# A table of rows in PSUM, a third step shared by two engines, and matrices made inside another step

## The chip, the cores and the metric

The kernel runs on one core of a Trainium2 chip. The core has a matrix engine (TensorE, "PE" in the profile), three engines for elementwise work (VectorE "DVE", ScalarE "ACT", GpSimd "POOL") and an engine whose queue here issues nearly all transfers (SyncE, "SP"). Matrix products land in PSUM, a small memory of eight banks; GpSimd does not touch it in this program. The metric is the time of one execution on the device, in microseconds. The program has one launch and computes everything from the raw inputs.

## The reference

Two blocks follow each other. The first is a long convolution over a sequence of 12480 positions, for a batch of 4 and 128 channels, done in the reference by FFT. The second is a feed-forward block over the 49920 rows that come out of it.

```python
h_mlp = np.maximum(pos_emb @ w1, 0.0) @ w2
h_filt = h_mlp * np.exp(-0.01 * pos)[:, None]
u = x * v
y = irfft(rfft(u, n=2*S) * rfft(h_filt, n=2*S))[:, :S, :]
attn = x * y                              # (4, 12480, 128)
x2 = attn.reshape(4 * 12480, 128)
h = x2 @ w_in                             # 128 -> 2048
out = (h * np.cos(h)) @ w_out             # 2048 -> 128
```

All values are float32.

## The kernel before

**The convolution.** The sequence is laid out as 104 rows (R) of 120 columns (N2), and the two transforms are products with small matrices of cosines and sines. For each of the four batch members there are four steps. In the forward first step (f1_units) and second step (f2_units) the product of x and v is transformed and multiplied with the filter. The third step (i1_units, 64 units) starts the way back. The fourth, the last inverse (i2_units), works in 30 groups (NG) of four columns: for each column two matrices of 96x104 stand against the third step's result in `slots`, and the product with x gives four columns of output rows, `zs`, which go to DRAM as `zd`.

**The third step.** One unit is four matmuls of 120x120 (L476, two records each) into one of eight banks, and its eviction i1_evict (L481). ScalarE copies half of the bank to SBUF (`other`, L484, a pool of two buffers); VectorE then writes the sum and the difference of the bank's other half and that copy to `slots` (L486, two instructions). Every inverse matmul of the fourth step reads all 64 units, so the fourth step cannot start before the last eviction.

For the first batch member the third step runs before the feed-forward block has begun, in the function `beside`: it is a generator that yields 130 times, and at every 14th yield a piece of w_out is converted from float64 words to float32 (convert_units: VectorE, GpSimd and ScalarE by turns), at every other fifth yield one matrix of the fourth step is made (some_groups).

**The matrices of the fourth step.** The two matrices of a column n2 are a rotation of the same table `rows` (96 x 4 x 104) by that column's cosine and sine from `tw_t` (make_t L305, turn L282). ScalarE writes the first term (L291). Then either VectorE adds the second term in one instruction (L293, scalar_tensor_tensor), or ScalarE writes the second term to `spare` (L296) and GpSimd adds the two (L297). make_group (L642) makes the four columns of a group and stores them to DRAM (`td`), where the other three batch members load them. For the first member, the groups in `SOME` (2, 7, 12, 17, 22, 27) are made by some_groups beside the third step, all on ScalarE and GpSimd, and loaded later; the other 24 are made within the fourth step, one group ahead of their use, two columns by VectorE (even ones) and two by GpSimd (odd ones). Group 0 is made when some_groups ends and advances the fourth step's generator once (L657).

**The feed-forward block** runs in 98 blocks of up to 128 x 4 rows with 16 steps each (1568 MoE steps). A step is a matmul up (L737, to a bank `ph` of four), then ScalarE `a` (L740), VectorE `k` (L743), GpSimd `f` (L746), ScalarE `cs` (L751), VectorE `gt` (L753), and four steps later a matmul down (L762, into `acc`). The cosine is made by `k`, `f` and `cs`.

**The order.** Nothing is reordered by a scheduler: every engine gets its instructions in the order in which the Python code emits them. The main loop emits a MoE step and then as many parts of the convolution's generators as fit its price (`owed`); one part of the first member's fourth step costs 0.875 MoE steps, a group has four parts, so groups carry 3 or 4 MoE steps by turns. `units` (L524) lays out a group: at part 0 the first half of its matmuls, the eviction of the group before, and the first column of the next group; at part 2 the second half. Beside it u_units of the next batch member runs (loads of x and v, L392, L398).

PSUM after the third step: one bank for `acc`, four for `ph`, three (`ps_c`) for the convolution.

Of the kernel before, what the change touches and what calls it, by code (L numbers as in the profile page):

```python
# [30 lines left out]
def kernel(  # L31
# [272 lines left out]

    def make_t(t, n2, **how):  # L305


        i = 1 if n2 < H - 1 else 0
        turn(t, rows[:, i:i + 2, :], rows[:, i + 1:i + 3, :], tw_t[:, 0, n2:n2 + 1],
             tw_t[:, 1, n2:n2 + 1], **how)  # L310
# [169 lines left out]

    def i1_evict(pool, ps, b):  # L481
        pj = ps[0:N1, 0:4 * N2].rearrange("p (i r j) -> p r j i", i=2, r=2)
        other = pool.tile([N1, N2, 2], F32, name="other")
        nc.scalar.copy(out=other[:, :, :], in_=pj[:, 1])  # L484
        for h, op in ((0, ALU.add), (1, ALU.subtract)):
            nc.vector.tensor_tensor(slots[0:N1, b, h * N2:(h + 1) * N2, :], pj[:, 0],  # L486
                                    other[:, :, :], op=op)
            yield
# [14 lines left out]

    def i2_out(pool, ps, xs, b, g):
        zs = pool.tile([R, 2, UA, D], F32, name="zs")
        nc.vector.tensor_tensor(
            zs[:, :, :, :].rearrange("p h n d -> p (h n d)"), ps[0:R, :],
            xs[:, :, :].rearrange("p h n -> p (h n)"), op=ALU.mult)
# [7 lines left out]
        yield  # L516

    made = [0]
    zbs = {}
# [3 lines left out]

    def units(n, steps, before, mm, after, parts, ahead=2):  # L524


        for j in range(min(ahead, n)):
            for _ in before(j) or ():
                pass
        yield 0.0  # L530
        last = iter(())
        for j in range(n):
            early = iter(before(j + ahead) or () if j + ahead < n else ())
            now = None
# [12 lines left out]
        for _ in last:  # L547
            pass
        yield REST

    SOME = range(2, NG, 5)
    REST = 3.0
# [77 lines left out]

    def i1_units(bank):
        with tc.tile_pool(name="mid", bufs=2) as pool:
            def mm(j, ps, i):
                if i == 0:
                    ps = bank()
                i1_mm(ps, j, i)
                return ps

            yield from units(CB, I1_STEPS, lambda j: None, mm,
                             lambda j, ps: i1_evict(pool, ps, j), 2)  # L640

    def make_group(pool, g, t, summed):  # L642

        for i, n2 in enumerate(n2s(g)):
            if summed < G and i % 2 == 0:
                make_t(t[:, i, :, :], n2)
            else:
                spare = pool.tile([N1, 2, R], F32, name="spare", bufs=2)
                make_t(t[:, i, :, :], n2, spare=spare[:, :, :])
            yield  # L650
        nc.sync.dma_start(td[g, :, :, :, :], t[:, :, :, :])

    def some_groups(pool):
        for g in SOME:
            t = pool.tile([N1, G, 2, R], F32, name="some", bufs=2)
            yield from make_group(pool, g, t, G)
        next(backs[0])  # L657

    def i2_units(bank, b, bufs):

        with tc.tile_pool(name="back", bufs=2, side="left" if b else "right") as pool:
# [10 lines left out]
            def mm(j, ps, i):  # L672
                if i == 0:
# [120 lines left out]
    with tc.manual_schedule():  # L794
        with tc.tile_pool(name="psum", bufs=8, space=PSUM) as psum, \
# [104 lines left out]
            nc.sync.dma_start(w_in_sb[:, :], wind[:, :])  # L900
            beside(i1_units(bank), [(w_out_sb[:, c, :], w) for c, w in out_pieces], some_groups)

        ps_acc = ctx.enter_context(tc.tile_pool(name="ps_acc", bufs=1, space=PSUM))
        ps_h = ctx.enter_context(tc.tile_pool(name="ps_h", bufs=4, space=PSUM))
        ps_c = ctx.enter_context(tc.tile_pool(name="ps_c", bufs=3, space=PSUM))
        mpool = ctx.enter_context(tc.tile_pool(name="moe", bufs=2))

        def bank():
            return ps_c.tile([P, BANK], F32, name="cv")
# [77 lines left out]
```

## Time and profile before

| What | us |
|---|---|
| median of four runs | 3773.79 (3771.79 to 3775.56) |
| the profiled execution: its time | 3772.35 |
| the profiled execution: its span | 3770.6 |
| third step of the first batch member (first to last matmul) | 272.7 to 333.5 |
| first inverse matmul | 338.3 |
| first matmul of the feed-forward block | 344.4 |
| last zs of the first member's fourth step starts | 586.5 |
| first matmul of the second member's forward step | 615.3 |

The span is what the profiler recorded on the core; the run's time is 1.75 us longer. A busy TensorE is not TensorE at its peak, since ends of matmuls are modelled: a record of 512 columns reads 592 ns, but in the chain of waits two of them take 0.86 us. float32 matmuls leave two records each.

The groups of the profile that the change touches, with the whole run's means:

| line, engine, what | count | mean ns |
|---|---|---|
| L486 VectorE, third step's sums and differences (first member) | 128 | 396 |
| L484 ScalarE, `other` (first member) | 64 | 346 |
| L293 VectorE, matrices within the fourth step | 48 | 941 |
| L297 GpSimd, matrices within the fourth step | 48 | 776 |
| L297 GpSimd, matrices beside the third step | 24 | 640 |
| L291 and L296 ScalarE, matrices | 192 | 455 to 468 |

### The profile page before, as it was taken

What the parts mean: (1) busy time and instruction counts of PE and PEld (TensorE: products, weight loads), DVE (VectorE), ACT (ScalarE), POOL (GpSimd) and SP (SyncE); (2) the same over time, 40 slices, a digit from 0 to 9 for tenths busy, and PEclk for the clock granted to TensorE, in tenths of its full rate; (3) what the DMA queues carried; (4) which work ended last, traced back from release to release, by engine and by line L of the source; (5) the groups of instructions that cost most, each with busy time, mean ns of one, the idle gap of its engine ahead of it and who ended that gap; (6) DMA issues with size and microseconds to landing.
All of it is one profiled execution on the core that took longest, in us unless ns stands there. A gap on an engine that the chain in (4) does not pass through costs nothing.

```text
span 3770.6 us, 47191 instructions
## 1 busy us (share of the span) xinstructions
PE 3692.9 (98%) x13546; PEld 2109.1 (56%) x13546; DVE 2779.2 (74%) x5562; ACT 2518.0 (67%) x4683; POOL 2570.3 (68%) x2342
## 2 busy tenths in 40 slices
PE   7898999999999999999999999999999999999999
PEld 6777555655566555555565556555566544444444
DVE  7887887688866777788766786788765566666666
ACT  5757776766665557766655567666664677777777
POOL 7667776588854665688745664788644577777776
PEclk9999999999999999999999999999999999999999
DMA  6263541022202550122103540122105200000000
GB/s 166 65 184 106 150 148 57 18 71 79 75 18 69 178 159 28 33 78 79 57 18 111 177 123 20 49 79 75 41 14 173 81 23 17 17 23 17 17 23 13
DMA packets 209499, 276.14 MB, mean 73 GB/s; under 512 B 17112, under 2 KB 146536, under 8 KB 209112
## 3 DMA queue, kind: packets, MB, share of 16 engines
q1 hardware_dynamic: 209239, 273.12, 24.5%
q8 instruction: 109, 1.79, 0.2%
q14 instruction: 151, 1.23, 0.1%
HBM read 193.64 MB, written 79.42 MB: 72 GB/s over the span
## 4 chain that ended last, share of the span: by engine, by line
PE 85%; DVE 4%; POOL 3%; DMA 3%; ACT 2%; issue 2%; SPq 0%; POOLq 0%; DVEq 0%; ACTq 0%
PE ph L737 33%; PE acc L762 28%; PE cv L501 5%; PE cv L762 5%; PE cv L476 4%; PE cv L445 3%; PE cv L404 3%; PE ph L126 2%; POOL f L746 2%; DMA hd<-h 2%; PE ps L404 1%; DMA tm<-td 1%; DVE slots L486 1%; ACT cs L751 1%; DVE gt L753 1%
## 5 line engine op out<-in xcount | busy, mean ns | idle before, releaser
L746 POOL TENSOR_TENSOR f<-a,k 128x512 f32<-128x512 f32 (+1 forms) x1568 | 1985.8, 1267 | 1059.9 <-DVE k L743 1056.0
L737 PE MATMUL ph<-at,w_in_sb 128*128 128x512 f32 (+1 forms) x3136 | 1599.0, 591 | 8.3 <-DVE gt L753 7.5
L740 ACT ACTIVATE a<-ph,quarter 128x512 f32<-128x512 f32 (+1 forms) x1568 | 1071.3, 683 | 687.2 <-PE ph L737 677.6
L762 PE MATMUL acc<-gt,w_out_sb 128*128 128x512 f32 (+1 forms) x2688 | 1370.0, 591 | 0.0
L753 DVE TENSOR_TENSOR gt<-ph,cs 128x512 f32<-128x512 f32 (+1 forms) x1568 | 1077.0, 687 | 368.6 <-ACT cs L751 353.4
L751 ACT ACTIVATE cs<-f 128x512 f32<-128x512 f32 (+1 forms) x1568 | 981.1, 626 | 385.5 <-POOL f L746 383.0
L743 DVE TENSOR_SCALAR k<-a 128x512 f32<-128x512 f32 (+1 forms) x1568 | 797.8, 509 | 545.3 <-ACT a L740 531.4
L762 PEld LDWEIGHTS acc<-gt,w_out_sb 128*128 128x128 f32 x2688 | 508.5, 189 | 642.0 <-issue 630.7
L737 PEld LDWEIGHTS ph<-at,w_in_sb 128*128 128x128 f32 x3136 | 553.0, 190 | 342.2 <-issue 261.6
L471 POOL TENSOR_TENSOR slots<-slots,t 120x256 f32<-120x256 f32 x384 | 311.3, 816 | 61.8 <-DVE t L464 25.8
L501 PEld LDWEIGHTS cv<-slots,tm 96*104 96x104 f32 x1920 | 239.6, 170 | 113.6 <-issue 84.3
L501 PE MATMUL cv<-slots,tm 96*104 96x128 f32 x1920 | 254.6, 274 | 13.7 <-DMA tm<-td 5.7
L762 PE MATMUL cv<-gt,w_out_sb 128*128 128x512 f32 (+1 forms) x448 | 224.6, 584 | 0.7 <-DVE gt L753 0.7
L476 PEld LDWEIGHTS cv<-cs,slots 120*96 120x96 f32 x1536 | 176.7, 167 | 67.6 <-issue 65.4
L476 PE MATMUL cv<-cs,slots 120*96 120x120 f32 x1536 | 183.1, 266 | 0.0
L445 PE MATMUL cv<-slots,w 124*120 124x256 f32 x576 | 173.1, 381 | 0.0
L445 PEld LDWEIGHTS cv<-slots,w 124*120 124x120 f32 x576 | 103.7, 184 | 123.7 <-issue 112.0
L404 PEld LDWEIGHTS cv<-c,slots 104*124 104x124 f32 x768 | 132.6, 192 | 71.2 <-issue 58.3
L404 PE MATMUL cv<-c,slots 104*124 104x192 f32 x768 | 151.2, 327 | 4.8 <-DVE gt L753 3.5
L762 PEld LDWEIGHTS cv<-gt,w_out_sb 128*128 128x128 f32 x448 | 84.9, 190 | 104.4 <-issue 99.4
L392 DVE TENSOR_TENSOR xt<-xt,vt 104x256 f32<-104x256 f32 x177 | 134.2, 761 | 0.2 <-DMA vt<-in_v_dram 0.2
L486 DVE TENSOR_TENSOR slots<-cv,other 96x240 f32<-96x240 f32 x384 | 133.1, 394 | 1.5 <-ACT other L484 1.4
(129 smaller groups left out, 2546.0 us busy)
## 6 DMA issues: line engine op xcount, KB each, us to landing
h<-hd SPq DMA_DIRECT2D x144, 240.0 KB
tm<-td SPq DMA_DIRECT2D x96, 312.0 KB
xt<-in_x_dram SPq DMA_DIRECT2D x120, 208.0 KB
vt<-in_v_dram SPq DMA_DIRECT2D x120, 208.0 KB
xs<-in_x_dram SPq DMA_DIRECT2D x120, 208.0 KB
zd<-zs SPq DMA_DIRECT2D x119, 208.0 KB
zb<-zd SPq DMA_DIRECT2D x96, 256.0 KB
w<-wd SPq DMA_DIRECT2D x144, 116.2 KB
```

Source lines behind the costliest of these rows:

```text
L404: nc.tensor.matmul(ps[0:KE, i * 2 * N1:(i + 1) * 2 * N1], u[:, b, 0:KE, i], c1[0:u.shape[0], :, :].rearrange("p r k -> p (r k)"), start=Tr ...
L445: nc.tensor.matmul(pi, w[:, i, :], parts[0:KE, :, k], start=True, stop=True)
L471: nc.gpsimd.tensor_tensor(y[:, r], y[:, r], t[:, r], op=op)
L476: nc.tensor.matmul(ps[0:N1, (i * 2 + r) * N2:(i * 2 + r + 1) * N2], parts[0:N2, r, :, b, i], cs[:, r, :], start=True, stop=True)
L501: nc.tensor.matmul(ps[0:R, i * D:(i + 1) * D], t[:, i, r, :], slots[0:N1, :, place, :], start=(r == 0), stop=(r == 1))
L737: nc.tensor.matmul(ph[:, 0:m], w_in_sb[:, c * P:(c + 1) * P], ats[n][:, 0:m], start=True, stop=True)
L740: nc.scalar.activation(a[:, 0:m], ph[:, 0:m], AF.Identity, bias=quarter[:, 0:1], scale=INV_TWO_PI)
L743: nc.vector.tensor_scalar(out=k[:, 0:m], in0=a[:, 0:m], scalar1=ROUND, scalar2=ROUND, op0=ALU.add, op1=ALU.subtract)
L746: nc.gpsimd.tensor_tensor(f[:, 0:m], a[:, 0:m], k[:, 0:m], op=ALU.subtract)
L751: nc.scalar.activation(cs[:, 0:m], f[:, 0:m], AF.Sin, scale=TWO_PI)
L753: nc.vector.tensor_tensor(gt[:, 0:m], ph[:, 0:m], cs[:, 0:m], op=ALU.mult)
L762: nc.tensor.matmul(accs[n][:, 0:m], w_out_sb[:, c, :], gt[:, 0:m], start=(c == 0), stop=(c == NFC - 1))
```

## The change

Six things are changed together.

- A copy of `rows` is put into a PSUM bank of its own by ScalarE, after the third step. make_t takes the second operand of VectorE's instruction from it, for the columns that VectorE makes. GpSimd's and ScalarE's part still reads SBUF. Group 0 is made before the copy exists and reads SBUF.
- That bank comes from the convolution's three, which has two until the first member's fourth step is over; then the table's pool is closed and three banks are opened.
- In the third step of the first member, units 58, 60 and 62 are evicted by GpSimd: ScalarE copies both halves of the bank to SBUF (`other` and `base`), GpSimd adds and subtracts. The other units stay as they were. i1_units of the later members passes no `last` and is unchanged.
- `SOME` has every seventh group (2, 9, 16, 23), four in place of six. Within the fourth step of the first member VectorE makes the odd columns and GpSimd the even ones.
- Before the last of the four groups, some_groups advances the fourth step's generator five times, so that group 0's four columns are made one by one within the third step. Conversions come at every 13th yield. To allow this, `units` yields while it prepares the first group, and inverse_units passes these yields on.
- In the first member's fourth step a group's matmuls come at parts 1 and 3 (`skip=1`), and its eviction one part later.

The program as a whole gets 3 `base` copies and one table copy on ScalarE, 6 adds on GpSimd in place of 6 on VectorE, 8 matrices made within the fourth step in place of beside the third, 50 of 52 L293 on tm with the PSUM operand, and 2 loads of `tm` fewer. The matmuls are the same.

```diff
-    def make_t(t, n2, **how):
+    def make_t(t, n2, copies=(), **how):
         i = 1 if n2 < H - 1 else 0
-        turn(t, rows[:, i:i + 2, :], rows[:, i + 1:i + 3, :], tw_t[:, 0, n2:n2 + 1],
+        second = rows
+        if copies:
+            second = copies[0]
+        turn(t, rows[:, i:i + 2, :], second[:, i + 1:i + 3, :], tw_t[:, 0, n2:n2 + 1],
              tw_t[:, 1, n2:n2 + 1], **how)
...
-    def i1_evict(pool, ps, b):
+    def i1_evict(pool, ps, b, gpsimd=False):
         pj = ps[0:N1, 0:4 * N2].rearrange("p (i r j) -> p r j i", i=2, r=2)
         other = pool.tile([N1, N2, 2], F32, name="other")
         nc.scalar.copy(out=other[:, :, :], in_=pj[:, 1])
+        first, engine = pj[:, 0], nc.vector
+        if gpsimd:
+            base = pool.tile([N1, N2, 2], F32, name="base")
+            nc.scalar.copy(out=base[:, :, :], in_=first)
+            first, engine = base[:, :, :], nc.gpsimd
         for h, op in ((0, ALU.add), (1, ALU.subtract)):
-            nc.vector.tensor_tensor(slots[0:N1, b, h * N2:(h + 1) * N2, :], pj[:, 0],
-                                    other[:, :, :], op=op)
+            engine.tensor_tensor(slots[0:N1, b, h * N2:(h + 1) * N2, :], first,
+                                 other[:, :, :], op=op)
             yield
...
     def i2_out(pool, ps, xs, b, g):
+        if b == 0:
+            yield
...
-    def units(n, steps, before, mm, after, parts, ahead=2):
+    def units(n, steps, before, mm, after, parts, ahead=2, skip=0):
         for j in range(min(ahead, n)):
             for _ in before(j) or ():
-                pass
+                yield 0.0
...
-                if i == 0 or 2 * i == max(parts, 2):
-                    now = mm(j, now, min(i, 1))
+                if i == skip or 2 * (i - skip) == max(parts, 2):
+                    now = mm(j, now, int(i > skip))
...
-    SOME = range(2, NG, 5)
+    SOME = range(2, NG, 7)
...
-                             lambda j, ps: i1_evict(pool, ps, j), 2)
+                             lambda j, ps: i1_evict(pool, ps, j, j >= CB - last and j % 2 == 0), 2)
...
-            if summed < G and i % 2 == 0:
-                make_t(t[:, i, :, :], n2)
+            if summed < G and i % 2:
+                make_t(t[:, i, :, :], n2, copies=rows_psum)
...
         for g in SOME:
+            if g == SOME[-1]:
+                for _ in range(G + 1):
+                    next(backs[0])
+                    yield
             t = pool.tile([N1, G, 2, R], F32, name="some", bufs=2)
             yield from make_group(pool, g, t, G)
-        next(backs[0])
...
-                             4 if b == 0 else 2, ahead=bufs - 1)
+                             4 if b == 0 else 2, ahead=bufs - 1, skip=int(b == 0))
...
-        for i, steps in enumerate(i2_units(bank, b, 2)):
+        back = i2_units(bank, b, 2)
+        for _ in range(0 if b else G):
+            yield next(back)
+        for i, steps in enumerate(back):
...
-                        if i % 14 == 0:
+                        if i % 13 == 0:
...
-            beside(i1_units(bank), [(w_out_sb[:, c, :], w) for c, w in out_pieces], some_groups)
+            beside(i1_units(bank, 6), [(w_out_sb[:, c, :], w) for c, w in out_pieces], some_groups)
...
-        ps_c = ctx.enter_context(tc.tile_pool(name="ps_c", bufs=3, space=PSUM))
+        stack = ctx.enter_context(ExitStack())
+        table_pool = stack.enter_context(tc.tile_pool(name="ps_t", bufs=1, space=PSUM))
+        two_banks = stack.enter_context(tc.tile_pool(name="ps_c", bufs=2, space=PSUM))
+        ps_c = [two_banks]
+        table = table_pool.tile([P, BANK], F32, name="table")
+        table = table[0:N1, 0:4 * R].rearrange("p (q n) -> p q n", q=4)
+        nc.scalar.copy(out=table, in_=rows[:, :, :])
+        rows_psum.append(table)
...
                 yield from backs[b]
+                if b == 0:
+                    stack.close()
+                    ps_c[0] = stack.enter_context(
+                        tc.tile_pool(name="ps_c", bufs=3, space=PSUM))
```

More of the change, by code (lines that the diff above doesn't have):

```diff
@@ L516, in i2_out @@
         yield
+    rows_psum = []
     made = [0]
     zbs = {}
-    def units(n, steps, before, mm, after, parts, ahead=2):
+    def units(n, steps, before, mm, after, parts, ahead=2, skip=0):
         for j in range(min(ahead, n)):
             for _ in before(j) or ():
-                pass
+                yield 0.0
         yield 0.0
@@ L629, in f2_both_units, with i1_units @@
             yield from units(N1 // 2, F2_STEPS, before, mm, after, 4, ahead=1)
-    def i1_units(bank):
+    def i1_units(bank, last=0):
         with tc.tile_pool(name="mid", bufs=2) as pool:
@@ L900 @@
             nc.sync.dma_start(w_in_sb[:, :], wind[:, :])
-            beside(i1_units(bank), [(w_out_sb[:, c, :], w) for c, w in out_pieces], some_groups)
+            beside(i1_units(bank, 6), [(w_out_sb[:, c, :], w) for c, w in out_pieces], some_groups)
         ps_acc = ctx.enter_context(tc.tile_pool(name="ps_acc", bufs=1, space=PSUM))
         ps_h = ctx.enter_context(tc.tile_pool(name="ps_h", bufs=4, space=PSUM))
-        ps_c = ctx.enter_context(tc.tile_pool(name="ps_c", bufs=3, space=PSUM))
+        stack = ctx.enter_context(ExitStack())
[6 more added lines that the diff above has]
+        rows_psum.append(table)
         mpool = ctx.enter_context(tc.tile_pool(name="moe", bufs=2))
         def bank():
-            return ps_c.tile([P, BANK], F32, name="cv")
+            return ps_c[0].tile([P, BANK], F32, name="cv")
         def convolutions():
```

## The prediction

> **What bounds the kernel now.** I read the page first: TensorE is busy for 98% of the span, so time can be won only where it idles or is slowed. The stage table shows where that is.
>
> ```profile
> PE 3692.9 (98%) x13546; PEld 2109.1 (56%) x13546; DVE 2779.2 (74%) x5562; ACT 2518.0 (67%) x4683; POOL 2570.3 (68%) x2342
> 272.00:333.50 61.50, 54.95 (x512) 53.07 (x512) 45.26 (x141) 38.62 (x120) 42.64 (x56) 1.00 0.27 85
> 333.50:338.30 4.80, 0.00 (x0) 0.00 (x0) 4.58 (x16) 4.23 (x14) 3.57 (x6) 0.78 0.07 20
> 338.30:344.40 6.10, 5.50 (x28) 5.30 (x28) 2.47 (x4) 3.34 (x9) 2.33 (x4) 0.61 0.76 218
> 372.60:586.50 213.90, 202.28 (x782) 112.64 (x781) 191.47 (x301) 154.47 (x306) 164.66 (x163) 1.00 0.50 149
> 616.00:3770.00 3154.00, 3142.27 (x10854) 1715.87 (x10852) 2266.26 (x4426) 2115.23 (x3661) 2127.40 (x1804) 1.00 0.21 62
> ```
>
> The columns are the stretch, its length, then TensorE, its weight loads, VectorE, ScalarE and GpSimd (each with a count), the granted clock, DMA share and GB/s. After 616 us TensorE idles 11.7 of 3154 us and runs at its own pace: whatever is won before 616 us comes off the end one for one, and nothing there is to be won. The change lies in two places before it: the end of the third step (272 to 344 us) and the first inverse (344 to 616 us), where VectorE is busy for 191.5 of 213.9 us.
>
> How much of the first inverse is lost is read from the starts of the zs multiplies (L506), one per group of matrices.
>
> ```profile
> 414.19 0.68 DVE L506 TENSOR_TENSOR zs<-cv,xs 104x512 f32<-104x512 f32 x1
> 424.07 0.68 DVE L506 TENSOR_TENSOR zs<-cv,xs 104x512 f32<-104x512 f32 x1
> 431.02 0.68 DVE L506 TENSOR_TENSOR zs<-cv,xs 104x512 f32<-104x512 f32 x1
> ...
> 466.74 0.68 DVE L506 TENSOR_TENSOR zs<-cv,xs 104x512 f32<-104x512 f32 x1
> 475.46 0.68 DVE L506 TENSOR_TENSOR zs<-cv,xs 104x512 f32<-104x512 f32 x1
> ```
>
> A group carries 3 or 4 MoE steps by turns. 414.19 to 424.07 is a four-step group beside which the next group's matrices are made: 9.88 us. 466.74 to 475.46 has four steps, but the next group is loaded (one of SOME): 8.72 us. The three-step pair is 7.95 (406.24 to 414.19) and 6.95 us (424.07 to 431.02). TensorE's own need is 4 x 1.72 + 16 x 0.111 = 8.66 and 3 x 1.72 + 1.78 = 6.94 us (0.43 us a record of 512 columns and 0.111 of 128, from the chain of waits: 0.86 for two, 0.89 for eight). So groups without making run at TensorE's pace, and making costs about 1 us a group. Summed over groups 5 to 29 (372.61 to 586.51 as ends), what lies over 8.72 and 6.95 is 18.7 us in 19 groups, 0.98 each. **This 18.7 us is what can be won there.**
>
> Why making costs it, VectorE's and GpSimd's groups in 372 to 587 us and one stretch of their timelines show:
>
> ```profile
> L743 DVE TENSOR_SCALAR k<-a 128x512 f32<-128x512 f32 x85 | 54.1, 636 | 8.0 <-ACT a L740 6.5 <-POOL f L746 1.3
> L293 DVE SCALAR_TENSOR_TENSOR tm<-rows,tw_t,tm 96x208 f32<-96x208 f32 x38 | 38.0, 1000 | 0.1
> L506 DVE TENSOR_TENSOR zs<-cv,xs 104x512 f32<-104x512 f32 x26 | 17.7, 680 | 0.0
> L297 POOL TENSOR_TENSOR tm<-tm,spare 96x208 f32<-96x208 f32 x39 | 30.9, 792 | 0.0
> ```
> ```profile
> 461.15 1.27 POOL L746 TENSOR_TENSOR f<-a,k 128x512 f32<-128x512 f32 x1 [0.99 <-DVE k L743]
> 462.38 0.80 POOL L297 TENSOR_TENSOR tm<-tm,spare 96x208 f32<-96x208 f32 x1
> 462.62 0.79 DVE L293 SCALAR_TENSOR_TENSOR tm<-rows,tw_t,tm 96x208 f32<-96x208 f32 x1
> 463.34 0.41 DVE L392 TENSOR_TENSOR xt<-xt,vt 104x256 f32<-104x256 f32 x1
> 463.68 0.41 DVE L743 TENSOR_SCALAR k<-a 128x512 f32<-128x512 f32 x1
> ```
>
> L293 needs 417 ns at best and takes up to 1617: it ends after the GpSimd add that was running. L506 (a PSUM operand) always takes 673 to 692 ns. GpSimd's L297 takes 792 ns here, 640 in the third step.
>
> The Trainium skill says it in the page "SBUF — State Buffer", section "Who interferes with whom": VectorE with two SBUF inputs and GpSimd reading SBUF exclude each other for a whole instruction, with one SBUF input they don't. The rows agree. By that rule alone L293 would lose all of its wait, the making its whole cost, and this stage 18.7 us.
>
> **The change, part by part.**
>
> Table in PSUM (make_t, L305). 50 of 52 L293 read one operand from PSUM. The nearest rows are L293 on w (124x120, one PSUM operand, 336 ns) and L486 (96x240, PSUM, 394 ns): about 0.37 us, 0.63 less, 1.26 for the two in a group. Not all of it is won. At 462.62 us the next instruction (L392) would need the port too and wait until L297 ends at 463.18, then end its turn near 463.5 instead of 463.68: some 0.2 of the 0.79. At 459.38 us L293 took 1.02, GpSimd was free at 460.17, and L398 would start 0.2 to 0.3 earlier. I take 0.25 for each L293, 0.50 a group; the bounds are 0.1 (the wait passes on) and 0.63. GpSimd's L297 also stops waiting for L293, at most 792 - 640 = 0.15 each; as L743 and L392 hold it up as well, I take half, 0.15 a group. A making group then costs 0.98 - 0.65 = 0.33 us (bounds 0 and 1.08).
>
> Fewer groups beside the third step: SOME falls from 6 to 4. In groups 5 to 28, 21 rather than 19 carry making (12 ScalarE, 4 VectorE, 4 GpSimd instructions move in, two tm loads go, two td stores change their place). New cost 21 x 0.33 = 6.9 us, so this stage gains 18.7 - 6.9 = **11.8 us**; bounds 18.7 and, at 1.08, a loss of 4.0. Groups 2 to 4 make too, with 416 columns and engines less full: 0 to 2 us, I take 0.7.
>
> Matmuls and zs one part later (skip=1, the extra yield): both move together, so two PSUM banks in place of three still leave as many parts between an eviction and the bank's next use, while a matrix has one part more before its matmul. That removes most of "PE cv L501 <- POOL tm L297", 2.9 us in seven waits, which is inside the 18.7. SP's order stays: the tm load still stands behind an xs load that waits for zs, so the 1.9 us wait for "DMA tm<-td" at 429.88 us can occur once (group 16) instead of twice (12 and 22).
>
> End of the third step. The timeline shows TensorE done at 333.47 and the last evictions at 337.95; VectorE is seven units behind, and the first inverse matmul needs them all.
>
> ```profile
> 332.43 1.04 PE L476 MATMUL ps<-cs,slots 120*96 120x120 f32 x8 [0.82 <-DVE slots L486]
> 331.56 2.61 DVE L486 TENSOR_TENSOR slots<-ps,other 96x240 f32<-96x240 f32 x8 [1.06 <-ACT other L484]
> 336.61 1.34 DVE L486 TENSOR_TENSOR slots<-ps,other 96x240 f32<-96x240 f32 x4
> 338.34 5.13 PE L501 MATMUL cv<-slots,tm 96*104 96x128 f32 x24 [4.88 <-DVE tm L293]
> ```
>
> VectorE needs 2.61/4 = 0.65 us a unit. GpSimd gets units 58, 60 and 62. "other" has two buffers, so those three units share one: the ScalarE copy for 60 waits until GpSimd has read 58's, and behind it in ScalarE's queue stand 61's copy and so VectorE. One link is 0.1 + 0.6 (two copies, 0.35 and 0.25 more) + 2 x 0.69 (between L297's 0.640 for 208 columns and L147's 0.727 for 256) = 2.1 us. With VectorE done with 56 at 332.9: copies to 333.6, GpSimd to 335.0, 337.1, 339.2, TensorE 0.4 later at 339.6, which is 1.3 after 338.34. Group 0's two L293 now stand ahead of it on VectorE (0.5 each), conversions and fewer makings pull the other way; I take **+1.5 us**. Bounds: -2.0 if GpSimd keeps VectorE's pace (three units off VectorE at 0.65), +3.0 with 0.82 an add (L471's mean) and both L293 in full.
>
> At nothing: the table copy on ScalarE (about 0.5 us, the 512-column copies take 0.574) and group 1's matrices, hidden behind group 0's 16 matmuls; without that cover 0.5. Group 0's making, hidden in the step. The reopening of three banks near 580 us, 30 us ahead of the first use.
>
> TensorE restarts at half pace: 0.213 us a record, clock 0.61 in 338.3 to 344.4, after 4.88 us of idling; after 3.06 us at 269.6 it did not. I expect 6 us of idling, so no change. The Trainium skill ("TensorE: Matmul & The Clock Gate", Part 1) puts the limit near one idle window of 3.4 us. By it, a wait under 3.4 us would also save 24 x 0.10 = 2.4 us.
>
> **Sum.** -11.8 - 0.7 + 1.5 = -11.0 us. The profiled span of 3770.6 becomes 3759.6; its run took 3772.35 (1.75 more) and the median is 1.44 above that, so the median goes from 3773.8 to **3762.8 us**.
>
> **Rivals.**
> The port's wait passes on. L743 (636 ns here, 0.41 when free) also needs the port and comes after every L293. If a third of the relief survives, a making group costs 0.98 - 0.22 = 0.76, the stage gains 18.7 - 16.0 = 2.7, and the sum with +1.5 is -1.2: 3772.6 us. For it speaks that L743's wait is as long as L293's; against it, that L293 itself holds GpSimd up.
>
> The GpSimd chain becomes the bound (slower). It is at 165 of 214 us, keeps both L297 of every group and gets six adds at the end of the third step. If making keeps its 0.98 us, 21 groups cost 20.6 (+1.9), the tail +3.0: 3778.7 us. It decides from 0.85 us a group, where 18.7 + 0.7 - 1.5 = 21 x 0.85. Against it: GpSimd idles 45 us for k alone in this stage.
>
> TensorE's wait falls below 3.1 us (the longest that the trace shows without a slower clock): GpSimd keeps pace (-2.0) and 2.4 us of half clock go, -16.9 in all: 3756.9 us. Two buffers of "other" speak against it.
>
> **Chances.** Forecast 0.58, with its own range 3757 to 3768; port wait passed on 0.26; GpSimd bound 0.08; short wait 0.08. A measurement can tell about 0.2%, 7.5 us: faster means below 3766.2. Of the forecast 0.54 lies there, with the short wait 0.62; slower takes most of the upper half of the GpSimd case, 0.05; the rest, 0.33, is the same. The range 3756 to 3772 leaves out the GpSimd case, the upper part of the passed-on wait and a little below.
>
> **What would show it.** L293 on tm at 0.35 to 0.45 us; making groups at 9.0 to 9.2 and 7.2 to 7.4 us between zs multiplies; L297 under 0.75; TensorE's wait before the first L509 at 5.5 to 7 us with the clock still low after it. Wrong if L293 stays above 0.6, if L743 grows by what L293 loses, or if making groups stay above 9.6.

## The result, and the profile after

The changed kernel takes 3767.95 us (median of 41 runs, 3763.64 to 3774.74) against 3772.65 us (61 runs, 3769.24 to 3779.26) of the kernel before on the same chips. The ratio is 0.9987, 95% interval 0.9982 to 0.9991: 4.9 us less (3.4 to 6.8), worked out with 3773.8. That is inside the 0.2% that the prediction called no change, so the class with the chance 0.33 came, not the one with 0.62; the time lies inside the range. In what follows a ratio is turned into microseconds in the same way.

The profiled execution took 3771.38 us, 3.4 above its median, and its span is only 1.1 us shorter than that of before. The whole run says little, then, and the stages say more. The page's first part and the stage table of after (stretch, length, then TensorE, weight loads, VectorE, ScalarE, GpSimd, granted clock, DMA share, GB/s; the first three stretches are cut at the same events as in the prediction's table, the fourth runs from the zs of group 4 to that of group 28):

```profile
PE 3695.2 (98%) x13546; PEld 2110.9 (56%) x13546; DVE 2770.6 (74%) x5560; ACT 2517.1 (67%) x4683; POOL 2582.8 (69%) x2344
272.00:331.70 59.70, 55.68 (x508) 53.98 (x506) 46.54 (x142) 37.48 (x115) 39.97 (x51) 0.97 0.28 87
331.70:337.20 5.50, 0.00 (x0) 0.02 (x1) 2.15 (x6) 2.06 (x8) 4.06 (x7) 0.67 0.18 58
337.20:344.00 6.80, 6.16 (x29) 5.84 (x29) 1.55 (x3) 3.16 (x8) 1.51 (x3) 0.50 0.32 97
374.00:573.00 199.00, 193.42 (x761) 109.48 (x762) 186.88 (x295) 150.66 (x307) 170.43 (x162) 1.00 0.51 155
```

The third step ends 1.8 us earlier (331.7 for 333.5), but it also begins 1.9 us earlier. Its first matmul in before, then in after (start, duration; in brackets the idle time before it, and what ended it):

```profile
272.68 0.45 PE L476 MATMUL ps<-cs,slots 120*96 120x120 f32 x2 [3.06 <-POOL slots L471]
```
```profile
270.82 0.45 PE L479 MATMUL ps<-cs,slots 120*96 120x120 f32 x2 [3.06 <-POOL slots L474]
```

Ahead of this point the change touches only the place of the conversions beside the first step, and eleven of the traces (after, e1 to e6 and e8 to e11 below) belong to kernels that are the same up to it: the step begins between 269.7 and 274.3 us in them. So what happens at its end is measured from its own first matmul. The first inverse matmul comes 66.38 us after it, before 65.66; the wait behind the step is 5.53 us, before 4.88.

The stretch from zs 4 to zs 28 takes 199.0 us where it took 206.95 (372.61 to 579.56). The prediction's row of before runs on to zs 29; up to zs 28 it is this one, and VectorE is no less busy in after (186.9 us for 185.2):

```profile
372.61:579.56 206.95, 195.62 (x764) 109.61 (x763) 185.21 (x291) 149.77 (x298) 159.80 (x159) 1.00 0.50 150
```

Where the next group's matrices are made, the multiplies zs of after mostly come in steps of 6.74 and 10.26 us by turns:

```profile
490.14 0.67 DVE L516 TENSOR_TENSOR zs<-cv,xs 104x512 f32<-104x512 f32 x1
496.89 0.68 DVE L516 TENSOR_TENSOR zs<-cv,xs 104x512 f32<-104x512 f32 x1
507.15 0.68 DVE L516 TENSOR_TENSOR zs<-cv,xs 104x512 f32<-104x512 f32 x1
```

With the eviction one part later a pair of groups is split differently, so only pairs compare: 17.0 us here, 17.8 before (9.88 and 7.95).

VectorE's and GpSimd's groups over the stretch (count, busy us, mean ns, idle before them) show what the table did. First before, from 372.61 to 579.56 us (its L293, 38 at 1000 ns, is in the prediction), then after, from 374 to 573 us. L761 is the k of before's L743, L395 and L401 its L392 and L398:

```profile
L743 DVE TENSOR_SCALAR k<-a 128x512 f32<-128x512 f32 x82 | 52.5, 640 | 7.7 <-ACT a L740 6.3 <-POOL f L746 1.3
...
L392 DVE TENSOR_TENSOR xt<-xt,vt 104x256 f32<-104x256 f32 x36 | 25.3, 706 | 0.0
...
L398 DVE TENSOR_TENSOR slots<-xt 104x256 f32<-104x256 f32 x24 | 13.4, 557 | 0.0
```
```profile
L761 DVE TENSOR_SCALAR k<-a 128x512 f32<-128x512 f32 x82 | 60.4, 737 | 3.1 <-ACT a L758 1.9
...
L395 DVE TENSOR_TENSOR xt<-xt,vt 104x256 f32<-104x256 f32 x36 | 31.8, 884 | 0.0
L401 DVE TENSOR_TENSOR slots<-xt 104x256 f32<-104x256 f32 x24 | 20.2, 841 | 0.0
L293 DVE SCALAR_TENSOR_TENSOR tm<-table,tw_t,tm 96x208 f32<-96x208 f32 x42 | 17.7, 421 | 0.3
```
```profile
L297 POOL TENSOR_TENSOR tm<-tm,spare 96x208 f32<-96x208 f32 x41 | 39.0, 952 | 0.6 <-ACT spare L296 0.6
```

L293 fell from 38.0 us (38 at 1000 ns) to 17.7 (42 at 421). But k went from 640 to 737 ns, the load's multiply from 706 to 884, the slots copies from 557 to 841, and GpSimd's L297 from 792 to 952. On VectorE 20.3 us were freed, and the three other lines, with as many instructions as before, took 21.2 us more (7.9, 6.5 and 6.8). The timeline shows how that goes (start, duration):

```profile
468.25 0.42 DVE L293 SCALAR_TENSOR_TENSOR tm<-table,tw_t,tm 96x208 f32<-96x208 f32 x1
468.65 0.92 DVE L761 TENSOR_SCALAR k<-a 128x512 f32<-128x512 f32 x1
```
```profile
468.01 1.27 POOL L764 TENSOR_TENSOR f<-a,k 128x512 f32<-128x512 f32 x1
```

L293 now runs inside GpSimd's f, which before it had to await. The k behind it needs 0.42 us when nothing stands against it, starts as soon as L293 is done, and ends at 469.57, 0.29 after f: it has inherited the wait. The whole trace agrees. Of the 24 L293 in after that start while an f has more than 0.45 us to run, none outlasts it; in e1 below, the same order without the table, all 29 do. From 374 to 573 us 20 k start while an f has more than 0.5 us to run, and all 20 outlast it, though k reads only one operand from SBUF.

At the end of the third step, PE, GpSimd and VectorE by the timeline:

```profile
329.77 1.91 PE L479 MATMUL ps<-cs,slots 120*96 120x120 f32 x17
337.21 5.42 PE L509 MATMUL cv<-slots,tm 96*104 96x128 f32 x24 [5.53 <-DVE slots L494]
```
```profile
332.02 1.33 POOL L494 TENSOR_TENSOR slots<-base,other 96x240 f32<-96x240 f32 x2
334.07 1.33 POOL L494 TENSOR_TENSOR slots<-base,other 96x240 f32<-96x240 f32 x2 [0.72 <-ACT base L491]
336.13 1.34 POOL L494 TENSOR_TENSOR slots<-base,other 96x240 f32<-96x240 f32 x2 [0.72 <-ACT base L491]
```

```profile
336.34 0.72 DVE L494 TENSOR_TENSOR slots<-ps,other 96x240 f32<-96x240 f32 x2 [1.34 <-ACT other L487]
```

GpSimd's chain of three sets the end. One link is 2.05 us, of which GpSimd idles 0.72 while ScalarE makes the next copies; and VectorE's last unit, which ends 0.15 us before TensorE starts, had to wait 1.34 us for a copy that stands in ScalarE's queue behind those. The last add's recorded end, 337.47, lies past TensorE's start; recorded ends on GpSimd are rough.

### The profile page after: what moved, and what is told of

Read it like the earlier page. It is cut to its first block, busy times and chain, and to the rows that moved or that the text cites. A ratio compares the mean times of both kernels' runs of the same rounds, so it can differ in the third digit from the quotient of the medians.

```text
span 3769.5 us, 47209 instructions
## 1 busy us (share of the span) xinstructions
PE 3695.2 (98%) x13546; PEld 2110.9 (56%) x13546; DVE 2770.6 (74%) x5560; ACT 2517.1 (67%) x4683; POOL 2582.8 (69%) x2344
## 4 chain that ended last, share of the span: by engine, by line
PE 86%; DVE 4%; POOL 3%; DMA 2%; ACT 2%; issue 2%; SPq 0%; POOLq 0%; DVEq 0%; ACTq 0%
PE ph L755 33%; PE acc L780 28%; PE cv L780 5%; PE cv L509 5%; PE cv L479 4%; PE cv L407 3%; PE cv L448 3%; PE ph L126 2%; POOL f L764 2%; PE ps L448 1%; DMA tm<-td 1%; PE ps L407 1%; DVE k L761 1%; PE ps L479 1%; ACT cs L769 1%
## 5 line engine op out<-in xcount | busy, mean ns | idle before, releaser
L761 DVE TENSOR_SCALAR k<-a 128x512 f32<-128x512 f32 (+1 forms) x1568 | 793.6, 506 | 560.9 <-ACT a L758 546.0
L395 DVE TENSOR_TENSOR xt<-xt,vt 104x256 f32<-104x256 f32 x177 | 140.5, 796 | 0.3 <-DMA vt<-in_v_dram 0.2
```

The costliest lines, as they stand in the source:

```text
L761: nc.vector.tensor_scalar(out=k[:, 0:m], in0=a[:, 0:m], scalar1=ROUND, scalar2=ROUND, op0=ALU.add, op1=ALU.subtract)
```

## The experiments

None of the twelve changes what is computed. The first theory was the prediction's own (the table wins the stage, the tail costs a little); its rivals: that the port's wait passes on, that GpSimd's chain bounds the end of the step, that the slow clock is what is paid. All ratios are to the kernel before, run beside each on the same chip; four chips were used, so ratios compare from row to row and medians do not. Each has 5 to 11 executions.

| run | us, median | ratio | 95% interval |
|---|---|---|---|
| e1_no_table | 3779.19 | 1.0016 | 1.0008 to 1.0025 |
| e2_tail_vector | 3765.82 | 0.9982 | 0.9973 to 0.9991 |
| e3_all_vector | 3756.11 | 0.9955 | 0.9943 to 0.9968 |
| e4_warm | 3765.37 | 0.9980 | 0.9971 to 0.9989 |
| e5_skip0 | 3765.22 | 0.9980 | 0.9971 to 0.9989 |
| e6_even | 3766.22 | 0.9984 | 0.9975 to 0.9993 |
| e7_before_table | 3763.49 | 0.9975 | 0.9966 to 0.9984 |
| e8_vector_warm | 3753.11 | 0.9950 | 0.9936 to 0.9963 |
| e9_bufs | 3763.73 | 0.9970 | 0.9958 to 0.9982 |
| e10_vector_skip0 | 3751.38 | 0.9938 | 0.9926 to 0.9951 |
| e11_vector_some2 | 3751.37 | 0.9937 | 0.9925 to 0.9950 |
| e12_before_vector | 3752.72 | 0.9951 | 0.9938 to 0.9965 |

**e1: the change without the table.** L293 reads `rows` in SBUF again; the copy stays, unread.

```diff
-        if copies:
-            second = copies[0]
```


> The changed kernel, but every L293 reads its second operand from SBUF again (the table is still copied, nobody reads it). If the table frees VectorE by what the prediction said (0.65 us in each of 21 groups), the time goes from 3768 to about 3781. If the wait for the port only moved to the instructions behind L293 (the profile of the changed kernel has k at 737 instead of 636 ns, the loads' multiply at 884 instead of 709, GpSimd's L297 at 952 instead of 792), most of it was given back: 3770 to 3774, with L293 back at 0.9 to 1.0 us and k and L297 back at 0.64 and 0.79. If the later place of the matmuls (skip=1) made the gain, no change: 3768.

Measured 1.0016: the new order without the table is slower than the kernel before, and the table is worth 1.0016 - 0.9987, 10.9 us, within the change. VectorE's and GpSimd's groups, 374 to 573 us:

```profile
L293 DVE SCALAR_TENSOR_TENSOR tm<-rows,tw_t,tm 96x208 f32<-96x208 f32 x40 | 48.9, 1224 | 0.3
L759 DVE TENSOR_SCALAR k<-a 128x512 f32<-128x512 f32 (+1 forms) x80 | 38.0, 475 | 2.0 <-ACT a L756 1.8
...
L297 POOL TENSOR_TENSOR tm<-tm,spare 96x208 f32<-96x208 f32 x40 | 40.2, 1004 | 0.0
```

Here L293 takes all the waiting and k little (475 ns); with the table it is the other way round (421 and 737). L297 is slow in both, so its 952 ns come with the new order and not with the table.

**e7: the kernel before with the table alone.** The bank, the copy, `copies` in make_t and the reopening of three banks; everything else as before.

```diff
-                make_t(t[:, i, :, :], n2)
+                make_t(t[:, i, :, :], n2, copies=rows_psum)
```


> The kernel before, with nothing but the table in PSUM and its bank (two banks for the convolution until the first inverse is over). By the prediction's sum for the table alone 19 groups gain 0.65 us: 12 us less than before, about 3760. If the table's worth comes from the new order only (where L293 without it took 1.22 us rather than 1.00), the gain is smaller: 3765 to 3768. If the port's wait passes on wholly, 3771 to 3772.

Measured 0.9975, 9.4 us (6.0 to 12.8) less than before: the table by itself brings more than the whole change (4.9). The rest of the change costs 4.5 us (0.0012 of 3773.8; with the two intervals taken as independent, 0.7 to 8.3).

```profile
L747 DVE TENSOR_SCALAR k<-a 128x512 f32<-128x512 f32 (+1 forms) x85 | 52.0, 611 | 10.4 <-POOL f L750 5.4 <-ACT a L744 4.3
L395 DVE TENSOR_TENSOR xt<-xt,vt 104x256 f32<-104x256 f32 x37 | 38.0, 1030 | 0.0
...
L293 DVE SCALAR_TENSOR_TENSOR tm<-table,tw_t,tm 96x208 f32<-96x208 f32 x37 | 15.6, 421 | 0.1
```

The wait passes on here too, but to the load's multiply (1030 ns, 706 before) and not to k (640 before). From zs 4 to zs 28 (198.17 us) VectorE is busy for 175.4 us where it was for 185.2: of the 22.0 us by which L293 is shorter there, some 12 come back on the lines behind it.

**e3: every matrix of the fourth step by VectorE** (group 0's even columns excepted), so that GpSimd's L297 and the copies into `spare` go.

```diff
-            if summed < G and i % 2:
+            if summed < G and (i % 2 or g):
```


> The changed kernel, with all four columns of a group within the fourth step made by VectorE from the table: 50 L297 (0.95 us each) and 50 L296 go, VectorE gets 50 more L293 at 0.42 (21 us over 29 groups). If what making still costs (0.49 us a group) is the contest for the port, which L297 takes part in and L293 with the table does not, the groups fall to TensorE's pace: 21 x 0.4 = 8 us less, about 3760. If VectorE's own work is the bound there (busy for 200 of 214 us), the groups grow by up to 0.3 us: 3768 to 3775.

Measured 0.9955, 17.0 us less than before. The stage table's row and two zs multiplies:

```profile
374.00:573.00 199.00, 199.00 (x786) 113.36 (x786) 177.30 (x345) 149.70 (x274) 149.74 (x126) 1.00 0.52 158
```
```profile
370.00 0.68 DVE L516 TENSOR_TENSOR zs<-cv,xs 104x512 f32<-104x512 f32 x1
...
559.80 0.68 DVE L516 TENSOR_TENSOR zs<-cv,xs 104x512 f32<-104x512 f32 x1
```

TensorE is busy without a gap, so zs 4 to zs 28 in 189.80 us is its own pace. That is a floor measured where the prediction had to work one out: 17.15 us could be won between these two events (206.95 - 189.80), and after won 7.95. VectorE does twice the matrices (80 of L293) and is less busy than in after (177.3 for 186.9): with GpSimd's adds gone, k is back at 482 ns. So VectorE's own work was not what was dear. Two readings of the rest are left: the contest for the port, and the place that L297 takes in GpSimd's queue ahead of f (39.0 us of adds in after), for e3 removes both together. No run took the adds off GpSimd and kept the contest.

**e2, e9 and e4: the end of the third step.** e2 gives the three units back to VectorE; e9 keeps them and gives `other` four buffers; e4 keeps all and lets five unread matmuls run in the wait.

```diff
-            beside(i1_units(bank, 6), [(w_out_sb[:, c, :], w) for c, w in out_pieces], some_groups)
+            beside(i1_units(bank, 0), [(w_out_sb[:, c, :], w) for c, w in out_pieces], some_groups)
```


> The changed kernel, with all 64 units of the third step evicted by VectorE. If the three GpSimd units form a chain (each waits for the buffer of the one before: links of 2.05 us in the profile), VectorE alone needs 6 x 0.65 = 3.9 us from 331.5 and the first inverse matmul comes at about 335.8 instead of 337.2: 1.5 us less, 3 us less if TensorE's clock then falls for a shorter time: 3765 to 3766.5. If GpSimd's share is a help, the first inverse matmul comes later, up to 2 us: 3768 to 3770.


```diff
-        other = pool.tile([N1, N2, 2], F32, name="other")
+        other = pool.tile([N1, N2, 2], F32, name="other", bufs=4)
```


> The changed kernel, with four buffers of the third step's copy (other) instead of two, so that a GpSimd unit no longer waits for the one before. If the buffer makes the chain, the six adds (0.67 us each) run on end from 332.0 and the first inverse matmul comes 1.4 us earlier: 3766.5, close to leaving GpSimd out (3765.8). If GpSimd's own pace and not the buffer sets the end, no change: 3768.


```diff
             beside(i1_units(bank, 6), [(w_out_sb[:, c, :], w) for c, w in out_pieces], some_groups)
+            warm = bank()
+            for _ in range(5):
+                nc.tensor.matmul(warm[:, :], ident[:, :], w_in_sb[:, 0:BANK], start=True, stop=True)
```


> The changed kernel, with five matmuls of 128x512 that nobody reads, issued on TensorE between the third step's last matmul and the first inverse matmul, where it waits for 5.5 us (4.3 us of work at full clock). If the half clock after that wait (24 records of the first groups at 0.22 instead of 0.11 us, records of 416 columns at double length until 347 us) is what costs, the time falls by 3 to 5 us: 3763 to 3765, and the clock is 1.0 from 338 to 347. If ScalarE and the chain of the first MoE steps set the pace there, no change: 3767 to 3769.

From the third step's first matmul to the first inverse matmul it takes 66.38 us in after, 64.26 in e2 and 62.81 in e9. GpSimd and TensorE of e9:

```profile
329.93 3.93 POOL L494 TENSOR_TENSOR slots<-base,other 96x240 f32<-96x240 f32 x6
```
```profile
333.85 4.52 PE L509 MATMUL cv<-slots,tm 96*104 96x128 f32 x24 [4.27 <-DVE slots L494]
```

Six adds run back to back, and the wait behind the step falls from 5.53 to 4.27 us, by 1.26 where 1.4 was expected. So the pool of two made the chain, as the prediction said. e9 is 6.4 us (1.6 to 11.2, the two intervals taken as independent) below after. Not all of that is the chain: the four buffers serve all 64 units, and the step itself is shorter, 58.55 us from its first matmul to its last for 60.85 in after and 60.51 in e2. The wait is still 0.52 us longer than e2's 3.75. Whether three units on GpSimd are a gain against VectorE alone, both with four buffers, was not tried. e2's gain of 1.9 us against after lies within its interval. e4's timeline:

```profile
331.78 4.46 PE L922 MATMUL ps<-w_in_sb,ident 128*128 128x512 f32 x10
337.49 3.12 PE L509 MATMUL cv<-slots,tm 96*104 96x128 f32 x24 [1.24 <-DVE slots L494]
```

The first 24 records of the inverse take 3.12 us where they took 5.42, and the clock stays at 1.00. The gain by ratio is 2.6 us, near the 2.4 that the prediction worked out, but inside the interval.

**e5 and e6: one part later, and the columns exchanged.** e5 sets skip to 0 and drops i2_out's extra yield; e6 gives VectorE the even columns again.

```diff
-                             4 if b == 0 else 2, ahead=bufs - 1, skip=int(b == 0))
+                             4 if b == 0 else 2, ahead=bufs - 1, skip=0)
```


> The changed kernel, with matmuls and evictions of a group back at parts 0 and 2 (skip=0, no extra yield); table, columns and SOME as changed. The prediction gave the later place a gain inside the groups (one part more between making and use, some 3 us of waits for L297): 3771. If the later place puts L293, the loads' multiply and L297 into each other's way (L297 took 0.95 us in the changed kernel, 0.79 before), undoing it helps: 3763 to 3766, with L297 nearer 0.8. If neither, 3768.


```diff
-            if summed < G and i % 2:
+            if summed < G and i % 2 == 0:
```


> The changed kernel, with VectorE on the even columns and GpSimd on the odd ones, as before. If the swap of the columns is what made L297 and the port's users slower, the time falls by 2 to 5 us, to 3763 to 3766, and L297 falls to about 0.8; if the swap is indifferent, 3767 to 3769, with L297 at 0.95.

By their times neither is told apart from after (2.6 and 1.1 us less, within the intervals). L297 takes 797 ns in e5 and 896 in e6, for 952. The stage shows more. The exchange of the columns costs there: e6, which undoes it, goes from zs 4 to zs 28 in 196.16 us, where the four traces with the odd columns and the same groups (after, e2, e4, e9) take 199.0 to 199.9:

```profile
371.95 0.68 DVE L516 TENSOR_TENSOR zs<-cv,xs 104x512 f32<-104x512 f32 x1
...
568.11 0.68 DVE L516 TENSOR_TENSOR zs<-cv,xs 104x512 f32<-104x512 f32 x1
```

e5, with the odd columns and skip=0, takes 200.33. What e5 wins comes later; TensorE's waits after 650 us in after, and then in e5 (total us, times, longest):

```profile
PE cv L509 <- DMA tm<-td: 6.8, 6, 1.9
```
```profile
PE cv L509 <- DMA tm<-td: 2.7, 4, 1.2
```

Before has 2.3 us there. A table over all traces, one execution of each kernel, shows the same throughout. "Ahead at the hand-over" is how much earlier than in before (612.03 us; the 615.3 in the table of times before the change is their second batch, 615.14) the second member's first forward matmul starts, less 1.7 us (two pairs of records at 0.86) where one MoE step fewer has been done by then; "ahead at the end" compares the spans with 3770.6. Both carry the chance start of the third step (before 272.68, after 270.82 us); the last column, their difference, does not.

| kernel | skip | ahead at the hand-over | ahead at the end | lost between |
|---|---|---|---|---|
| after | 1 | 7.3 | 1.1 | 6.2 |
| e1 / e2 / e3 | 1 | 1.2 / 10.5 / 19.7 | -2.9 / 6.0 / 16.3 | 4.1 / 4.5 / 3.4 |
| e4 / e6 / e8 | 1 | 10.0 / 12.2 / 20.7 | 5.3 / 5.4 / 17.7 | 4.7 / 6.8 / 3.0 |
| e9 / e11 | 1 | 12.8 / 24.8 | 8.8 / 21.0 | 4.0 / 3.8 |
| e5 / e7 | 0 | 9.2 / 9.2 | 7.6 / 9.0 | 1.6 / 0.2 |
| e10 / e12 | 0 | 21.8 / 21.5 | 20.1 / 19.5 | 1.7 / 2.0 |

All nine kernels with skip=1 lose 3.0 to 6.8 us after the hand-over, the four with skip=0 lose 0.2 to 2.0. The waits for td there are 4.0 to 6.8 us in the nine and 2.2 to 2.9 in the four. The run times do not separate it: the two pairs that differ in this alone, after and e5, e8 and e10, lean the same way by 2.6 and 4.5 us, within their intervals. Why the phase of the first member's matmuls makes TensorE wait longer for the other members' td loads was not tried.

**e8, e10, e11, e12: towards a faster version.** e8 is e3 with VectorE's tail (e2) and three unread matmuls; e10 is e8 with skip=0; e11 is e8 with one group beside the third step in place of four; e12 is the kernel before with the table, e3's columns and the three matmuls, and nothing else.

```diff
-    SOME = range(2, NG, 7)
+    SOME = range(2, NG, 28)
```


> The changed kernel, with three things together that each helped alone: VectorE makes all four columns of a group within the fourth step, VectorE evicts all units of the third step, and three unread matmuls of 128x512 keep TensorE busy in the wait that is left (3.75 us). If the gains are independent (11.8, 2.1 and 2.6 us, the last one smaller as the wait is shorter), 3751 to 3753; if the clock after the wait and the tail are the same gain, 3754; if they overlap wholly, 3756.

> VectorE makes all columns, VectorE evicts all third-step units, three unread matmuls in the wait, and the matmuls and evictions of a group back at parts 0 and 2. If the later place costs by the phase that it gives the later batch members (waits for tm<-td of 4 to 7 us after 660 us in all kernels with it, 2 to 3 in those without) and by the slower clock after the wait of 1.86 us near 600 us, undoing it wins 2 to 3 us here too: 3750 to 3751. If its cost lay in the port's contest inside the groups, which is gone here, no change: 3753.

> VectorE makes all columns, VectorE evicts all third-step units, three unread matmuls in the wait, and only group 2 is made beside the third step (SOME has one group instead of four). If a group made by VectorE from the table costs nothing on the path (groups at 9.10 and 6.92 us, TensorE idle 0.00 us from 350 to 570), the three groups moved in cost nothing, and the third step, which VectorE and ScalarE bound, gets up to 2 us shorter: 3751 to 3753. If their 18 ScalarE and VectorE instructions a group still cost 0.3 us each group, 3754.

> The kernel before with the table, all matrices of the fourth step by VectorE (group 0's odd columns excepted), and three unread warm-up matmuls ahead of the first inverse matmul; nothing else of the change: six groups beside the third step, group 0 made behind it, third step evicted by VectorE alone, matmuls at parts 0 and 2. It differs from e10 by SOME and by the place of group 0's matrices alone (and the column that group 0 gives to VectorE). Theory 'the table is the whole of the gain, and the rest of the change adds nothing': as e10, 0.9938 of the time before, 3750 to 3752 us, groups at TensorE's floor (heavy and light together 16.05 us). Theory 'fewer groups beside the third step and group 0's matrices made inside it do bring forward the first inverse matmul': 2 to 4 us slower than e10, 3753 to 3755, with the first inverse matmul later than e10's by as much and no difference in the groups. If it were faster than e10 (below 3749), the two steps would cost time even there.

e10 and e11 are the fastest, 23.4 and 23.8 us below before (18.5 to 28.3 with both intervals), and faster than both kernels of the case. e12 gets 18.5 us without the order of the change; the 4.9 us by which its ratio is above e10's are not separated by the intervals. Its zs 0 starts at 339.60 and its hand-over is at 590.52, e10's at 339.84 and 590.27, but its third step began 1.9 us earlier (271.00 for 272.92). From there e10 is 1.7 us ahead at zs 0 and 2.2 us at the hand-over. So fewer groups beside the step and making group 0 inside it may be worth some 2 us, by one trace of each. e11, with still fewer groups beside the step, has a shorter step than e8 (58.38 us from first to last matmul for 60.98) and its first inverse matmul 2.8 us sooner after the step's start (61.94 for 64.74); their ratios are 4.9 us apart, within the intervals.

```profile
331.36 2.75 PE L908 MATMUL ps<-w_in_sb,ident 128*128 128x512 f32 x6
336.54 4.54 PE L504 MATMUL cv<-slots,tm 96*104 96x128 f32 x24 [2.44 <-POOL tm L297]
```

In e12 group 0's matrices are ready only 2.4 us after the warming matmuls, and the clock falls all the same (4.54 us for the records that took 2.88 in e10).

## Why the prediction was right or wrong

**What could be won: right.** It said 18.7 us between zs 4 and zs 29; e3's gapless stretch gives 17.15 between zs 4 and zs 28, and e10, the fastest, gains 17.1 up to zs 29 (196.8 us for 213.9).

**What a making group still costs: mis-sized.** The step was "A making group then costs 0.98 - 0.65 = 0.33 us". By e3's floor, 19 groups cost 17.15/19 = 0.90 before, 8.4/19 = 0.44 with the table alone (e7: zs 4 to zs 28 in 198.17) and 9.2/21 = 0.44 in after. The stage gained 7.95 us for the 11.8 forecast. Two things make it up: the ceiling was 1.5 lower, and each of 21 groups kept 0.11 more. In the new order the second is the exchange of the columns, which the sum gave no price: with the even columns, in e6's one trace, a making group costs 6.4/21 = 0.30.

With the table alone the cost fell by 0.46 us a group: 0.23 for each of the two L293 if it is all theirs, where 0.25 was put. The 0.15 from a faster L297 was wrong: the table alone took it from 792 to 773 ns (0.04 us a group), and in the change it rose to 952. The first rival, that the port's wait passes on, describes what VectorE shows (21.2 us more on three lines for 20.3 freed), and k's growth was the prediction's own sign of being wrong. But of the 0.65 us a group 0.46 reached the path and not a third, and the stage's 7.95 us lie nearer to the forecast's 11.8 than to the rival's 2.7. That k and the loads have slack that L293 had not would explain it; no run shows that.

Of the other signs, L293 at 0.42 us came as forecast, L297 under 0.75 did not, and four-step groups of 10.26 us are past the 9.6 that was to prove it wrong, though as pairs (17.0 us) they stand between before's 17.8 and the forecast's 16.2 to 16.6. The page "SBUF — State Buffer" of the Trainium skill, section "Who interferes with whom", has VectorE instructions with two SBUF inputs and GpSimd's reads of SBUF exclude each other for a whole instruction. L293 agrees, 421 ns inside f with one input in SBUF and 1224 with two; the 18.7 us that the prediction worked out from that rule alone did not come.

**Early groups: nothing, for 0.7 us.** Groups 2 to 4, from zs 1 to zs 4, take 22.30 us before and 22.52 after. The group ahead of them takes 10.59 us for 8.19: in this execution the granted clock was 0.50 from 340 to 345 us and 0.78 from 345 to 350, in before 0.70 and 1.00.

**End of the third step: mechanism right, size too large.** Forecast +1.5. The first inverse matmul comes 1.1 us earlier counted from the start of the execution (338.34 to 337.21), but the step had begun 1.9 us earlier by chance. From the step's first matmul it comes 0.7 us later (65.66 to 66.38), and from its last 0.65 us later: the wait is 4.88 us in before and e7, and 5.53 or 5.54 in all six kernels with the three units on GpSimd and two buffers. The link was put at 2.1 us and is 2.05, and the cause, two buffers, is shown by e9. What was too large is the tail of the chain: TensorE was to start 0.4 us after the last add and started 0.26 before its recorded end. At the first feed-forward matmul after is 1.4 us behind (71.76 to 73.13 from the step's start): the half clock lasted past 345 us in this execution, where it was to stay as it was.

**Waits for GpSimd and for td: right in the stage, wrongly credited.** "PE cv <- POOL tm L297" is gone and the td wait before the hand-over came once, 0.9 us. But the first wait is gone with the table and skip=0 too (e5, e7), and with skip=1 and no table (e1): either removes it, so beside the table skip=1 had little left to win in the stage (200.33 us in e5, 199.0 to 199.9 with it).

**"Whatever is won before 616 us comes off the end one for one": failed.** This is the step that cost most in the profiled pair. It holds for the table alone (9.2 us at the hand-over, 9.0 at the end) and not for the change: 7.3 became 1.1, and 1.9 of either is the earlier start of the third step. Of the 6.2 lost, 4.5 are waits for td after 650 us (6.8 for 2.3) and some 1.7 a clock of 0.83 from 600 to 610 us. The prediction costed skip=1 by the stage in which it acts; in the traces its price is paid in the stage after. By the ratios 4.9 us are left, so a typical execution is likely to lose less than this profiled one; which of the two losses varies was not told apart. The rival of the short wait took 3.1 us as a wait without a slower clock; after's own trace has the clock at 0.66 for 5 us behind a wait of 3.06 (at 270.82 us), so that limit was one execution's chance.

**The sum.** The prediction's terms make -12.4 us for the table alone (19 groups of the old order at 0.65) and so +1.4 for all the rest; the runs give -9.4 and +4.5. Both terms were about 3 us too hopeful, and the sum is -4.9 where -11.0 was forecast. The direction was right, the size less than half. The errors went the same way and did not cancel; the time lies inside the range because the range also covered a change of next to nothing.

## What to carry to other kernels

Taking one user off a contended resource is worth what the next user in line cannot take back: count who queues behind it, and measure the floor of the stage by a kernel that drops the contention altogether. A part of a combined change should be tried alone first: here the table with its bank, two of the six parts, brought more than all six. A shift of phase is to be priced in the stage that follows, at the waits for transfers, not only where it acts. And a stage of one trace is compared with that of another from the stage's own start: here starts differed by more than what was sought.

## What the runs showed of the hardware

The clock's fall does not follow from the length of a wait alone. At the hand-over TensorE waits 1.86 us in all nine kernels with skip=1, behind nearly the same instructions. The stage table's rows around it, of after (wait at 601.2 to 603.0 us) and then of e9 (595.7 to 597.6):

```profile
590.00:600.00 10.00, 10.00 (x24) 4.29 (x23) 9.31 (x15) 5.79 (x10) 7.91 (x8) 1.00 0.18 56
600.00:610.00 10.00, 8.14 (x23) 4.27 (x22) 7.43 (x14) 4.91 (x9) 7.95 (x8) 0.83 0.28 75
```
```profile
590.00:600.00 10.00, 8.13 (x21) 3.48 (x21) 8.20 (x13) 4.31 (x8) 8.17 (x9) 1.00 0.18 48
600.00:610.00 10.00, 9.51 (x38) 5.99 (x37) 8.12 (x18) 8.31 (x17) 6.14 (x6) 1.00 0.14 46
```

The clock fell in six of them (after, e1, e2, e3, e4, e6) and stayed at 1.00 in three (e8, e9, e11); with a wait of 1.47 or 1.48 us it stayed in all five. After the third step it fell for waits of 2.44 us (e12) and more. At the start of that step TensorE waits 3.05 to 3.48 us in all fourteen traces: the clock stayed at 1.00 in four (before, e1, e6, e10) and fell in ten (0.50 to 0.70 over the next 5 us). The Trainium skill's page "TensorE: Matmul & The Clock Gate", Part 1, has an activity window that runs free of the program, which would let the same wait fall inside or across one. That one and the same wait has both outcomes agrees with it, while its length of about 3.4 us is more than the 1.86 us after which the clock fell here.

Runs of one kernel differ with the clock granted over the whole run: of after's, the eight with a mean clock of 0.994 have a mean span of 3769.4 us, the 21 with 0.995 one of 3765.6, the 12 with 0.996 one of 3764.6; a single one with 0.993 has 3767.8. The profiled execution is one of the eight.
